# Fused attention and two gated layers: three raw-weight buffers, a single A22 buffer and weight units made at other steps

## The chip, the cores and the metric

The kernel is one program on one core of a Trainium2 chip. The metric is the device time of one execution in microseconds (us), from three runs. Engines are named as in the profile: PE (TensorE matmul), DVE (VectorE), ACT (ScalarE), POOL (GpSimd), SP (the engine whose queue issues the DMAs).

## The reference, cut to what matters

Three layers follow each other on 2304 tokens. The change lies in the third.

```
x  = attention(q, k, v, bias from positions)          # 4 x 8 heads, 576 positions, depth 64
h  = x @ w_in;  x = (h * cos(h)) @ w_out              # 512 -> 2048 -> 512
xn = x / sqrt(mean(x*x) + 1e-6) * rms_g
g, val = xn @ w_gate, xn @ w_val                      # 512 -> 1536, twice
out = (g / (1 + exp(-g)) * val) @ w_out               # 1536 -> 512
```

The weights arrive as 64-bit floats. On the chip each is made into a 32-bit float and then into a high and a low part, and each product is three matmuls (high by high, high by low, low by high).

## The kernel before

**Weights.** A piece is 128 x 512 weights, 512 KB raw. `w_dma` (L105) loads it on SP's queue into one of `NRAW` = 2 raw buffers. `w_abs` (L112, ACT) takes the absolute value of its upper words into one of `NW32` = 6 buffers named `w`. `w_conv` finishes it on DVE in four quarters (L123, L125, L127, L129); the last one frees the raw buffer, and `w_load` then asks for the next piece. Six pieces (two of gate, two of val, two of out) make a group.

**The third layer** runs in twelve groups, `run_group(p)`: groups 0 to 5 over 1024 tokens, 6 to 11 over 1024 others. A band of 256 tokens ("short") is fitted between in groups 1 to 5 and 7. In a group the gate and val products are seven products of half-sized blocks each (`gP1` to `gP7`, `vP1` to `vP7`, L974, six matmuls); `D0` to `D7` and `E0`, `E1` multiply what the group before made with its out weights (L1103, six matmuls), and `S0` to `S3` are the short products (L974 and L1078, tile `sh`). `steps(p)` fixes their order, in groups 2 to 5: gP1 gP2 D0..D7 E0 E1 vP1 vP2 gP6 gP7 vP6 vP7 S0 S1 gP5 vP5 gP3 S2 gP4 vP3 S3 vP4.

**Weight units.** In groups 0 to 5 the high and low parts, and sums of blocks, are made while the products run: `make` writes `g0 g1 g2 v0 v1 v2 o0 o1` and `gA`, `vA` (block A22, needed by P4 alone) with `halves` (a cast on ACT, L811, then a subtraction on POOL, L812), and `gS`, `vS` are four POOL operations in place (L927). `build` makes the first unit of a queue if its pieces are converted and its place is free, one per step. A22 has two buffers, `a0` and `a1`. The places are ten slots `wA`, `wB`, `wC`. `keep` stores each made unit to memory, from where groups 6 to 11 load it, so these make nothing.

**After a product**, `after` copies its sums out of PSUM on ACT, adds on DVE (`sums`, L1010) and multiplies (`times`, L986); `halves` makes the gated result `g` (ACT, then POOL). P3 adds into the same PSUM tile (`R`) that P5 filled, so gP3 waits for DVE's sum after gP5.

**Between them** stands a list `background`, one entry per step, for the 1/rms scaling of tokens that later groups use (blocks 2, 3 and 4): squares (ACT, L724) and their sums (DVE, L728), `rms_sum` (PE transposes into tile `sh`, shown as `ssp`, L734), `rms_mean` (DVE, then twelve small POOL operations, L749 to L752), `rms_back` (PE transposes into `sh`, shown as `rbp`, L759, and a copy to `rb` on ACT, L761), `rms_xn` (DVE, L766). `fit` and `mix` (L808) form operands for groups 6 to 11 in group 5, by the table `later2`.

What runs at a step of groups 0 to 5 is set in this order: the product, `after`, the table, `keep`, `build`, then `w_fill` (how many quarters is in `FILLS`), then `w_abs`:

```
x = wstate["abs"]
if x < wstate["dma"] and x < wstate["splitd"] + NW32 and tick[0] - asked.get(x, 0) >= 5:
    w_abs()
```

`tick` advances by 2 at a product and by 1 at other steps. Each engine works off its own list in order.

## Time and profile before

| | |
|---|---|
| median of 3 runs | 1179.1 us (1179.09 to 1179.51) |
| profiled execution | 1179.42 us |
| its span, first to last instruction | 1177.6 us |
| PE busy | 1123.0 us, 95% |
| DVE, ACT, POOL busy | 874.3, 606.7, 539.4 us |
| mean granted TensorE clock | 0.987 |

The page's slices show PE at 9 tenths or more nearly everywhere but between about 680 and 975 us, where it falls to 7 and 8; the granted clock dips to 8 in two slices there. That stretch is groups 0 to 5. A row of a timeline gives the start, the duration, the engine, line and operation with its tiles, and in brackets how long the engine had been idle and what ended it.

### The profile page before, as it was taken

Reading aid. Unit: us, or ns where it says so; the run is one execution under the profiler, and the core shown is the slowest. Engines: PE = TensorE matmul, PEld = TensorE weight load, DVE = VectorE, ACT = ScalarE, POOL = GpSimd, SP = SyncE. Lnnn points to the kernel's source line nnn. Section 1 sums busy time; section 2 is a strip of 40 time slices with the busy share of each in tenths; the row PEclk is TensorE's granted clock in tenths of the full one; section 3 lists DMA queues with packets and bytes.
Section 4 is the critical chain, followed back from the end, with each engine's and each line's share of the span. In section 5 each row is a group of like instructions: output and inputs, shape, how many; then the busy total and the mean of one; then the engine's idle time right before and its main releaser. Section 6 shows DMA issues by size and latency. Waiting matters only on the chain. (4 is left out here: it accounts for less than half of the span.)

```text
span 1177.6 us, 18893 instructions
## 1 busy us (share of the span) xinstructions
PE 1123.0 (95%) x6748; PEld 893.3 (76%) x6748; DVE 874.3 (74%) x1577; ACT 606.7 (52%) x1217; POOL 539.4 (46%) x649
## 2 busy tenths in 40 slices
...
GB/s 257 281 88 213 106 205 112 208 119 79 60 54 1 37 54 54 19 54 58 15 54 36 55 72 142 182 112 208 144 173 186 53 1 122 118 155 177 156 148 90
DMA packets 54286, 131.22 MB, mean 111 GB/s; under 512 B 8912, under 2 KB 15824, under 8 KB 54192
## 3 DMA queue, kind: packets, MB, share of 16 engines
...
q0 software_dynamic: 1584, 1.46, 0.8%
...
## 5 line engine op out<-in xcount | busy, mean ns | idle before, releaser
L678 POOL TENSOR_TENSOR g<-t,g 128x512 fp32r<-128x512 f32 (+1 forms) x80 | 98.7, 1234 | 233.4 <-ACT g L677 233.3
L812 POOL TENSOR_TENSOR g<-t,g 128x512 fp32r<-128x512 f32 (+1 forms) x60 | 76.0, 1267 | 219.0 <-ACT g L811 214.8
L627 PE MATMUL y<-g,wB 128*128 128x512 f32 (+1 forms) x600 | 132.0, 369 | 1.1 <-DVE yacc L712 1.1
L627 PEld LDWEIGHTS y<-g,wB 128*128 128x128 f32 x600 | 105.0, 189 | 20.3 <-DVE yacc L712 1.5
L264 DVE CUSTOM_DVE_ANT_0 e<-psS,bias 128x576 f32<-128x576 f32 x144 | 103.5, 752 | 22.6 <-PE psS L250 20.7
L273 ACT ACTIVATE e<-e,sm 128x576 f32<-128x576 f32 x144 | 111.3, 773 | 11.3 <-DVE sm L264 11.3
L627 PE MATMUL h<-xh,wB 128*128 128x512 f32 (+1 forms) x360 | 109.1, 369 | 0.0
L672 ACT ACTIVATE r<-r 128x512 f32<-128x512 f32 (+1 forms) x80 | 47.2, 590 | 118.8 <-DVE r L669 118.4
L1103 PE MATMUL y<-wC,g 128*128 128x512 f32 x300 | 86.9, 397 | 8.6 <-DVE yacc L1010 6.1
L677 ACT CAST g<-t 128x512 fp32r<-128x512 f32 (+1 forms) x80 | 46.2, 578 | 92.4 <-DVE t L676 86.1
L974 PE MATMUL Rg<-xh,wB 128*128 128x512 f32 x192 | 71.7, 415 | 18.5 <-DVE r L1010 17.7
L1103 PE MATMUL y<-wA,g 128*128 128x512 f32 x300 | 85.1, 392 | 0.0
L327 PE MATMUL o<-eT,v 128*64 128x256 f32 (+1 forms) x640 | 84.7, 411 | 0.0
L627 PE MATMUL y<-g,wC 128*128 128x512 f32 (+1 forms) x360 | 81.0, 375 | 3.8 <-POOL g L678 3.8
L811 ACT CAST g<-t 128x512 fp32r<-128x512 f32 (+1 forms) x60 | 34.7, 578 | 95.5 <-DVE t L986 95.5
L250 PE MATMUL psS<-kt,qt 64*128 64x288 f32 (+1 forms) x810 | 80.7, 309 | 0.8 <-DVE sm L264 0.7
L1010 DVE TENSOR_TENSOR yacc<-y,yacc 128x512 f32<-128x512 f32 (+1 forms) x81 | 54.5, 682 | 35.6 <-PE y L1103 35.5
L250 PEld LDWEIGHTS psS<-kt,qt 64*128 64x128 f32 (+1 forms) x810 | 62.5, 185 | 23.7 <-issue 8.5
L676 DVE TENSOR_TENSOR t<-r,h 128x512 f32<-128x512 f32 (+1 forms) x80 | 50.4, 630 | 34.9 <-ACT r L673 34.3
L627 PEld LDWEIGHTS y<-g,wC 128*128 128x128 f32 x360 | 63.6, 193 | 16.2 <-POOL g L678 4.0
L627 PEld LDWEIGHTS h<-xh,wB 128*128 128x128 f32 x360 | 65.8, 188 | 12.4 <-POOL wB L148 0.6
L1103 PEld LDWEIGHTS y<-wC,g 128*128 128x128 f32 x300 | 56.0, 190 | 24.1 <-DVE yacc L1010 8.6
(192 smaller groups left out, 2835.8 us busy)
## 6 DMA issues: line engine op xcount, KB each, us to landing
raw<-in_wf_dram SPq DMA_DIRECT2D x68, 512.0 KB, 3.7
wB<-kept SPq DMA_DIRECT2D x27, 512.0 KB, 4.2
kept<-wB SPq DMA_DIRECT2D x25, 512.0 KB, 2.7
...
kept<-wC SPq DMA_DIRECT2D x15, 512.0 KB, 3.0
wC<-kept SPq DMA_DIRECT2D x14, 512.0 KB, 4.3
...
```

Of the source, the lines that this page charges most:

```text
L250: nc.tensor.matmul(ps[:, x, 0:288], qt[r, a, 128 * p:128 * p + 128], kt[r, b_, k0:k0 + 288], start=(n == 0), stop=(n == len(terms) - 1), t ...
L264: nc.vector.tensor_tensor_reduce(out=e.rearrange("p (a b) -> p a b", a=2), in0=ps[:, :, 0:288], in1=bias_t[j].rearrange("p (a b) -> p a b" ...
L273: nc.scalar.activation(e, e, AF.Exp, bias=s_["m"][:, j:j + 1], scale=-1.0, accum_out=s_["sum"][:, j:j + 1])
L327: nc.tensor.matmul(o[64 * hh:64 * hh + 64, 0:n], vt[:, c, 64 * hh:64 * hh + 64], eT[:, 2 * c + (hh if c < 4 else 0), :], start=(c == 0), s ...
L627: nc.tensor.matmul(ps, a, b_, start=(first and k == 0), stop=(last and k == tot - 1))
L672: nc.scalar.activation(r, r, AF.Abs)
L676: nc.vector.tensor_tensor(t, r, ps, op=ALU.mult)
L678: nc.gpsimd.tensor_tensor(g[:, 1, :tn], t, g[:, 0, :tn].bitcast(F32), op=ALU.subtract)
L812: (eng or nc.gpsimd).tensor_tensor(lo, x, hi.bitcast(F32), op=ALU.subtract)
L974: nc.tensor.matmul(ps, w[:, a, cols], x[b](kt), start=(start and k == 0), stop=(k == n - 1), skip_group_check=not start)
L1010: nc.vector.tensor_tensor(to, x, y, op=ALU.add)
L1103: nc.tensor.matmul(y, g[a], o[:, b, cs], start=(n == 0), stop=(n == 5))
```

## The change

- The raw buffers become three and the `w` buffers five. `tick` advances by 1 at every step, and an absolute value comes at least six steps after its load was asked for.
- 1/rms is read by `rms_xn` from the PSUM tile it was transposed into; in the third layer the copy to `rb` goes.
- A22 has one buffer: `gA` and `vA` of a group are made after the group before has used its A22. The units' order becomes g0 v0 gA gS vA vS g1 g2 v1 v2. Groups 0 to 5 use nine slots.
- No quarter of a conversion at D2, D5, D7 (before: none at odd ones); one where there is something to convert at the other D and E steps.
- `rms_sum` of blocks 3 and 4 runs at D4 to gP7 only, `rms_back` at D2 to vP1 only.
- In group 5, operands are formed at other steps; the low part of T3 is made on DVE, and block 4's temporary lies in the buffers of the squares.
- The first partial results of a token block are copied from PSUM by DVE at even D, by ACT at odd D (before: all by ACT).

```
--- before.py
+++ after.py
@@ -33,8 +33,8 @@
 WB = 6
 WC = 3
 RING = WA + WB + WC
-NRAW = 2
-NW32 = 6
+NRAW = 3
+NW32 = 5
 SPL = 0
 LAG = 2
 NTT = S // 16
@@ -757,8 +757,10 @@
         ps = turn_tile("rbp")
         for t in range(0, tn, 128):
             nc.tensor.transpose(ps[:, t:t + 128], rst[bi][:, t // 128:t // 128 + 1].to_broadcast([128, 128]), ident)
-        rst[bi] = env["mp2"].tile([128, 512], F32, tag="rb", name="rb", bufs=1)[:, :tn]
-        nc.scalar.copy(rst[bi], ps[:, :tn])
+        rst[bi] = ps[:, :tn]
+        if env["psX"] is None:
+            rst[bi] = mp.tile([128, 512], F32, tag="u", name="rb", bufs=2)[:, :tn]
+            nc.scalar.copy(rst[bi], ps[:, :tn])
 
     def rms_xn(bi, d):
         t0, tn = BLKS[bi]
@@ -802,7 +804,7 @@
             todo = [((b_[:, hi], b_[:, hi], a[:, lo]), (a[:, hi], a[:, hi], b_[:, hi]))[k - 2]]
         else:
             if k == 2:
-                t2[:] = [rawp.tile([128, 512], I32, tag="w32", name="t2", bufs=NW32).bitcast(F32) for _ in range(2)]
+                t2[:] = [env["mp2"].tile([128, 512], F32, tag="sq", name="t2", bufs=2) for _ in range(2)]
             todo = [((t2[i], b_[:, 2 + i], a[:, i]), (a[:, 2 + i], a[:, 2 + i], t2[i]))[k - 2] for i in range(2)]
         for to, x, y in todo:
             nc.vector.tensor_tensor(to, x, y, op=ALU.subtract)
@@ -861,13 +863,13 @@
     tick = [0]
     mixed = {}
     asked = {}
-    ROLES = ("g0", "a0", "v0", "g1", "g2", "v1", "v2", "o0", "o1", "a1")
+    ROLES = ("g0", "a0", "v0", "g1", "g2", "v1", "v2", "o0", "o1")
     wr = {}
     free = dict.fromkeys(ROLES, 0)
     built = []
     units = {"G": [], "O": []}
     for q in range(PAIRS):
-        units["G"] += [(k, q) for k in ("gA g0 gS vA v0 vS g1 g2 v1 v2" if q else "g0 gA vA gS v0 vS g1 g2 v1 v2").split()]
+        units["G"] += [(k, q) for k in ("g0 v0 gA gS vA vS g1 g2 v1 v2" if q else "g0 gA vA gS v0 vS g1 g2 v1 v2").split()]
         units["O"] += [(k, q) for k in ("o0", "o1")]
     released = set()
 
@@ -885,7 +887,7 @@
         x = 2 if k[0] == "v" else 0
         if k[0] == "o":
             return base + 4 + int(k[1]), (k,)
-        return {"A": (base + x + 1, ("a%d" % (q % 2),)), "S": (base + x + 1, ())}.get(k[1], (base + x, (k,)))
+        return {"A": (base + x + 1, ("a0",)), "S": (base + x + 1, ())}.get(k[1], (base + x, (k,)))
 
     CLOSE = ("gP3", "S2", "gP4", "vP3", "S3", "vP4")
     OPEN = ("vP7", "S0", "S1", "gP5", "D0", "D1", "D2", "D3", "D4", "D5", "D6", "D7", "E0", "E1")
@@ -900,7 +902,7 @@
                 continue
             if q and (name in CLOSE or k[1] == "S" and name and name not in OPEN):
                 continue
-            if piece >= wstate["convd"] or any(r not in wr or free[r] < (q - 1 if r[0] == "a" else q) for r in roles):
+            if piece >= wstate["convd"] or any(r not in wr or free[r] < q for r in roles):
                 continue
             units[queue].pop(0)
             make(k, q)
@@ -928,10 +930,10 @@
             mixed[m, q] = tick[0]
         elif k[1] == "A":
             c = hi if m == "v" else lo
-            t = wr["a%d" % (q % 2)]
+            t = wr["a0"]
             halves(t[:, 0, c], t[:, 1, c], b[:, hi])
             if m == "v":
-                built.append((tick[0], "a%d" % (q % 2), q))
+                built.append((tick[0], "a0", q))
         else:
             halves(wr[k][:, 0], wr[k][:, 1], a if k[1] == "1" else b)
             w32_t.pop(x + int(k[1]) - 1)
@@ -943,7 +945,7 @@
         while wstate["split"] in released:
             wstate["split"] += 1
 
-    kept = dramp.tile([PAIRS - 1, len(ROLES) - 1, 128, 2, 512], F32, name="kept")
+    kept = dramp.tile([PAIRS - 1, len(ROLES), 128, 2, 512], F32, name="kept")
 
     def keep():
         while built and tick[0] - built[0][0] >= 4:
@@ -986,10 +988,10 @@
         nc.vector.tensor_tensor(t, t, val, op=ALU.mult)
 
     def part_a(p):
-        return "a%d" % (p % 2 if p < PAIRS else 1)
+        return "a0"
 
     def store_of(role):
-        return ROLES.index("a0" if role == "a1" else role)
+        return ROLES.index(role)
 
     def strassen(p, m, name):
         w, c0, x, bank, start = P[name]
@@ -1107,7 +1109,7 @@
             else:
                 to = oacc[bi].rearrange("p (d x) b -> p d (x b)", x=2)[:, d, cs]
             if first:
-                nc.scalar.copy(to, y)
+                (nc.scalar.copy if d % 2 else nc.vector.tensor_copy)(to, y)
             else:
                 sums(to, y, to)
             if last:
@@ -1149,8 +1151,8 @@
 
     later2[0] = {"gP2": [(fit, 1, "T1", nc.vector)], "gP7": [(fit, 1, "T4")]}
     later2[PAIRS - 1] = {"vP1": [(fit, 4, "B11")], "vP2": [(mix, 4, 0)], "gP6": [(fit, 4, "B21"), (mix, 4, 2)],
-                         "vP6": [(mix, 4, 3)], "vP7": [(fit, 4, "T2")], "S1": [(mix, 4, 1), (fit, 4, "T3")],
-                         "S2": [(fit, 4, "T1")], "S3": [(fit, 4, "B22")]}
+                         "vP7": [(fit, 4, "T2")], "S0": [(mix, 4, 1)], "vP5": [(fit, 4, "T3", nc.vector)], "S2": [(fit, 4, "T1")],
+                         "vP3": [(mix, 4, 3)], "S3": [(fit, 4, "B22")]}
     later2[PAIRS] = {"gP1": [(fit, 4, "T4")]}
     def steps(p):
         down = [f"D{k}" for k in range(8)] * (p > 0) + ["E0", "E1"] * (p - 1 in SHORT_IN)
@@ -1174,7 +1176,7 @@
     def run_group(p):
         todo, frees = steps(p)
         for i, name in enumerate(todo):
-            tick[0] += 2 if "P" in name else 1
+            tick[0] += 1
             if name == "L":
                 item_down(NI - 1)
                 st_psY.close()
@@ -1194,9 +1196,9 @@
             if p <= PAIRS:
                 keep()
                 build(name)
-                w_fill(FILLS.get(name, 1 - int(name[1]) % 2 if name[0] in "DE" else 1) if p else 2 if i > 3 else 0)
+                w_fill(FILLS.get(name, 0 if name in ("D2", "D5", "D7") else 1) if p else 2 if i > 3 else 0)
                 x = wstate["abs"]
-                if x < wstate["dma"] and x < wstate["splitd"] + NW32 and tick[0] - asked.get(x, 0) >= 5:
+                if x < wstate["dma"] and x < wstate["splitd"] + NW32 and tick[0] - asked.get(x, 0) >= 6:
                     w_abs()
                 for k in ("abs", "conv", "split"):
                     wstate[k + "d"] = wstate[k]
@@ -1204,7 +1206,9 @@
                 w_load()
                 asked.update((y, tick[0]) for y in range(x, wstate["dma"]))
                 if (p > 0 or i > 3) and background and not (p > 1 and background[0][0] in (rms_add, rms_xn) and name[0] in "DE" and int(name[1]) % 2 == 0) and not (
-                        p in SHORT_IN and background[0][0] in (rms_sum, rms_back) and name in ("S0", "S1", "gP5", "vP5", "gP3", "S2", "gP4", "vP3", "S3", "vP4")):
+                        p in SHORT_IN and (
+                        background[0][0] is rms_sum and name not in ("D4", "D5", "D6", "D7", "vP1", "vP2", "gP6", "gP7") or
+                        background[0][0] is rms_back and name not in ("D2", "D3", "D4", "D5", "D6", "D7", "vP1"))):
                     fn, *a = background.pop(0)
                     fn(*a)
                     if fn is rms_sum:
```

**POOL, group 4, from the subtraction for v0 on** (gate weights' w buffers are the first pair, val's the second; `wB`, `wC` are slots). Before:

```order
L812 TENSOR_TENSOR wB<-w_9397,wB 128x512
L927 TENSOR_TENSOR w_9419<-w_9419 128x256
L927 TENSOR_TENSOR w_9419<-w_9397,w_9419 128x256
L927 TENSOR_TENSOR w_9397<-w_9419,w_9397 128x256
L927 TENSOR_TENSOR w_9397<-w_9397 128x256
L812 TENSOR_TENSOR wB<-w_9262,wB 128x512
L812 TENSOR_TENSOR wB<-w_9272,wB 128x512
L812 TENSOR_TENSOR wC<-w_9397,wC 128x512
L812 TENSOR_TENSOR wC<-w_9419,wC 128x512
```

The change:

```order
L814 TENSOR_TENSOR wB<-w_9385,wB 128x512
L814 TENSOR_TENSOR wB<-w_9264,wB 128x256
L929 TENSOR_TENSOR w_9264<-w_9264 128x256
L929 TENSOR_TENSOR w_9264<-w_9252,w_9264 128x256
L929 TENSOR_TENSOR w_9252<-w_9264,w_9252 128x256
L929 TENSOR_TENSOR w_9252<-w_9252 128x256
L814 TENSOR_TENSOR wB<-w_9421,wB 128x256
L929 TENSOR_TENSOR w_9421<-w_9421 128x256
L929 TENSOR_TENSOR w_9421<-w_9385,w_9421 128x256
L929 TENSOR_TENSOR w_9385<-w_9421,w_9385 128x256
L929 TENSOR_TENSOR w_9385<-w_9385 128x256
L814 TENSOR_TENSOR wB<-w_9252,wB 128x512
```

The subtraction for gA, the four operations of gS and that for vA, which stood in the group before at gP7, gP5 and vP5, now stand between v0 and vS: g1 (the last row here, the sixth before) has ten instructions between v0 and itself where it had four. Behind it stand, in groups 2 and 4, the twelve small operations of `rms_mean`, then g2, v1 and v2. (The change's own lines have numbers two higher from L766 on.)

**DVE, group 2, from gP6's two quarters to the sum after gP5** (`r<-Rg`, the last row; `t<-t,sh` is the short band's product at S1). Before:

```order
L127 SCALAR_TENSOR_TENSOR w_8887<-raw,w_8887 128x512
L129 SCALAR_TENSOR_TENSOR w_8887<-raw,w_8887 128x512
L123 TENSOR_SCALAR w_9004<-w_9004 128x512
L125 TENSOR_SCALAR w_9004<-w_9004 128x512
L728 TENSOR_TENSOR sq<-sq 128x512
L127 SCALAR_TENSOR_TENSOR w_9004<-raw,w_9004 128x512
L129 SCALAR_TENSOR_TENSOR w_9004<-raw,w_9004 128x512
L123 TENSOR_SCALAR w_9029<-w_9029 128x512
L728 TENSOR_TENSOR sq<-sq 128x512
L986 TENSOR_TENSOR t<-t,sh 128x256
L125 TENSOR_SCALAR w_9029<-w_9029 128x512
L1010 TENSOR_TENSOR r<-Rg,r 128x512
```

The change:

```order
L127 SCALAR_TENSOR_TENSOR w_8894<-raw,w_8894 128x512
L129 SCALAR_TENSOR_TENSOR w_8894<-raw,w_8894 128x512
L123 TENSOR_SCALAR w_8906<-w_8906 128x512
L125 TENSOR_SCALAR w_8906<-w_8906 128x512
L127 SCALAR_TENSOR_TENSOR w_8906<-raw,w_8906 128x512
L129 SCALAR_TENSOR_TENSOR w_8906<-raw,w_8906 128x512
L988 TENSOR_TENSOR t<-t,sh 128x256
L123 TENSOR_SCALAR w_9017<-w_9017 128x512
L1012 TENSOR_TENSOR r<-Rg,r 128x512
```

The two sums of squares are gone from here (block 4's now run in group 3), and so are three quarters: none is left at vP7 and S0.

**ACT, group 2, from the cast for g1 to the copy of vP1's result** (`r<-Rv`; `L112` are absolute values). Before:

```order
L811 CAST wB<-w_8506 128x512
L811 CAST wB<-w_8546 128x512
L112 ACTIVATE w_8865<-raw 128x512
L811 CAST wC<-w_8612 128x512
L112 ACTIVATE w_8887<-raw 128x512
L811 CAST wC<-w_8642 128x512
L761 COPY rb<-rbp 128x512
L1110 COPY yaccs<-y 128x512 x2
L1016 COPY r<-Rv 128x512
```

The change:

```order
L813 CAST wB<-w_8512 128x512
L813 CAST wB<-w_8554 128x512
L112 ACTIVATE w_8881<-raw 128x512
L813 CAST wC<-w_8655 128x512
L112 ACTIVATE w_8894<-raw 128x512
L813 CAST wC<-w_8682 128x512
L112 ACTIVATE w_8906<-raw 128x512
L1112 COPY yaccs<-y 128x512
L1018 COPY r<-Rv 128x512
```

Three absolute values stand behind the casts for g2, v1 and v2, where there were two, behind those for g2 and v1. With six `w` buffers they took the buffers that g1 and g2 had been made from; with five they take those of g1, g2 and v1. All stand ahead of the copy that vP2's sum on DVE needs. The copy to `rb` is gone, and of the two copies of first partial results one is left.

## Rows read from the trace of the kernel before

**Rows 1.** Windows, groups 0 to 5 and 7; length, then busy PE, PEld, DVE, ACT, POOL, clock.
```profile
698.52:728.98 30.46, 23.74 (x99) 18.22 (x99) 23.73 (x31) 16.52 (x32) 19.67 (x16) 0.93 0.44 150
728.98:780.82 51.84, 40.13 (x183) 31.32 (x182) 38.30 (x54) 25.60 (x51) 34.01 (x39) 0.93 0.49 166
780.82:832.30 51.48, 44.44 (x202) 36.58 (x200) 39.80 (x59) 22.51 (x43) 30.61 (x37) 0.90 0.51 168
832.30:883.46 51.16, 42.35 (x202) 34.29 (x200) 39.75 (x56) 18.70 (x36) 29.30 (x36) 0.97 0.48 159
883.46:924.32 40.86, 39.05 (x193) 32.62 (x192) 30.76 (x45) 17.65 (x34) 26.84 (x24) 1.00 0.50 169
924.32:972.34 48.02, 41.03 (x194) 33.51 (x192) 29.55 (x36) 19.95 (x37) 36.99 (x28) 0.96 0.00 1
...
1004.98:1040.72 35.74, 35.74 (x182) 30.52 (x180) 7.82 (x11) 13.84 (x25) 7.06 (x6) 1.00 0.40 130
```

**Rows 2.** PE's waits in 698.5:972.4; us in total, times, longest.
```profile
PE Rg L974 <- DVE r L1010: 17.7, 5, 5.0
PE y L1103 <- DVE yacc L1010: 6.1, 6, 1.2
PE ssp L734 <- DVE t L986: 5.9, 2, 3.1
PE Xv L974 <- ACT wC L811: 4.9, 1, 4.9
```

**Rows 3.** The chain that ended last, group 7; start, us, what.
```profile
1007.86 10.88 PE y L1103 x48
```

**Rows 4.** PE timeline, group 2: the squares' transposes behind gP1.
```profile
785.41 1.12 PE L734 MATMUL ssp<-ident,sq 128*128 128x128 f32 x4 [3.07 <-DVE t L986]
```

**Rows 5.** ACT timeline, group 2: two absolute values.
```profile
800.52 0.67 ACT L112 ACTIVATE w<-raw 128x512 f32<-128x512 f32 x1 [6.58 <-POOL wB L812]
...
819.15 0.66 ACT L112 ACTIVATE w<-raw 128x512 f32<-128x512 f32 x1 [1.73 <-DMA raw<-in_wf_dram]
```

**Rows 6.** DVE timeline, group 2: quarters that wait, and the sum behind one.
```profile
801.22 0.79 DVE L123 TENSOR_SCALAR w<-w 128x512 f32<-128x512 f32 x1 [3.46 <-ACT w L112]
...
819.84 0.43 DVE L123 TENSOR_SCALAR w<-w 128x512 f32<-128x512 f32 x1 [0.99 <-ACT w L112]
...
821.63 0.68 DVE L1010 TENSOR_TENSOR r<-Rg,r 128x512 f32<-128x512 f32 x1
```

**Rows 7.** The page, DMA issues: count, KB, us to landing.
```profile
raw<-in_wf_dram SPq DMA_DIRECT2D x68, 512.0 KB, 3.7
```

**Rows 8.** POOL timeline, group 4: last gate subtraction, v0, then g1 and g2.
```profile
889.76 1.73 POOL L812 TENSOR_TENSOR g<-t,g 128x512 fp32r<-128x512 f32 x1 [1.28 <-ACT g L811]
891.46 1.30 POOL L812 TENSOR_TENSOR wB<-w,wB 128x512 fp32r<-128x512 f32 x1
...
895.85 2.55 POOL L812 TENSOR_TENSOR wB<-w,wB 128x512 fp32r<-128x512 f32 x2
```

**Rows 9.** POOL timeline, group 3: first and last of rms_mean's twelve operations.
```profile
842.41 0.20 POOL L749 TENSOR_TENSOR rsm<-rsm 128x4 f32<-128x4 f32 x1 [0.31 <-DVE rsm L747]
...
845.50 0.20 POOL L752 TENSOR_TENSOR rsm<-rsm 128x4 f32<-128x4 f32 x1
```

**Rows 10.** POOL timeline, group 4: subtraction for a 256-wide unit, nothing beside it.
```profile
887.74 0.74 POOL L812 TENSOR_TENSOR g<-t,g 128x256 fp32r<-128x256 f32 x1 [1.39 <-ACT g L811]
```

**Rows 11.** DVE timeline, group 4: a quarter beside POOL, then a first and a last quarter alone.
```profile
907.88 1.68 DVE L129 SCALAR_TENSOR_TENSOR w<-raw,w 128x512 int32<-128x512 int32 x1
910.59 0.43 DVE L123 TENSOR_SCALAR w<-w 128x512 f32<-128x512 f32 x1 [1.04 <-ACT w L112]
...
912.66 0.69 DVE L129 SCALAR_TENSOR_TENSOR w<-raw,w 128x512 int32<-128x512 int32 x1
```

**Rows 12.** POOL timeline, group 4: what ran beside the quarter of 907.88.
```profile
907.51 1.49 POOL L812 TENSOR_TENSOR g<-t,g 128x512 fp32r<-128x512 f32 x1 [1.28 <-ACT g L811]
```

**Rows 13.** DVE timeline, group 5: the two operations of one mix.
```profile
956.21 3.44 DVE L808 TENSOR_TENSOR yacc<-yacc,t 128x512 f32<-128x512 f32 x2 [1.20 <-POOL xl L812]
```

More of the change, by code (lines that the diff above doesn't have):

```diff
@@ L35 @@
 RING = WA + WB + WC
-NRAW = 2
-NW32 = 6
+NRAW = 3
+NW32 = 5
 SPL = 0
@@ L759, in rms_back @@
             nc.tensor.transpose(ps[:, t:t + 128], rst[bi][:, t // 128:t // 128 + 1].to_broadcast([128, 128]), ident)
-        rst[bi] = env["mp2"].tile([128, 512], F32, tag="rb", name="rb", bufs=1)[:, :tn]
-        nc.scalar.copy(rst[bi], ps[:, :tn])
+        rst[bi] = ps[:, :tn]
+        if env["psX"] is None:
+            rst[bi] = mp.tile([128, 512], F32, tag="u", name="rb", bufs=2)[:, :tn]
+            nc.scalar.copy(rst[bi], ps[:, :tn])
     def rms_xn(bi, d):
@@ L804, in mix @@
             if k == 2:
-                t2[:] = [rawp.tile([128, 512], I32, tag="w32", name="t2", bufs=NW32).bitcast(F32) for _ in range(2)]
+                t2[:] = [env["mp2"].tile([128, 512], F32, tag="sq", name="t2", bufs=2) for _ in range(2)]
             todo = [((t2[i], b_[:, 2 + i], a[:, i]), (a[:, 2 + i], a[:, 2 + i], t2[i]))[k - 2] for i in range(2)]
@@ L869, in attn_moe @@
     for q in range(PAIRS):
-        units["G"] += [(k, q) for k in ("gA g0 gS vA v0 vS g1 g2 v1 v2" if q else "g0 gA vA gS v0 vS g1 g2 v1 v2").split()]
+        units["G"] += [(k, q) for k in ("g0 v0 gA gS vA vS g1 g2 v1 v2" if q else "g0 gA vA gS v0 vS g1 g2 v1 v2").split()]
         units["O"] += [(k, q) for k in ("o0", "o1")]
@@ L902, in build @@
                 continue
-            if piece >= wstate["convd"] or any(r not in wr or free[r] < (q - 1 if r[0] == "a" else q) for r in roles):
+            if piece >= wstate["convd"] or any(r not in wr or free[r] < q for r in roles):
                 continue
@@ L944, in release @@
             wstate["split"] += 1
-    kept = dramp.tile([PAIRS - 1, len(ROLES) - 1, 128, 2, 512], F32, name="kept")
+    kept = dramp.tile([PAIRS - 1, len(ROLES), 128, 2, 512], F32, name="kept")
     def keep():
@@ L1109, in down @@
             if first:
-                nc.scalar.copy(to, y)
+                (nc.scalar.copy if d % 2 else nc.vector.tensor_copy)(to, y)
             else:
@@ L1151, in attn_moe @@
     later2[PAIRS - 1] = {"vP1": [(fit, 4, "B11")], "vP2": [(mix, 4, 0)], "gP6": [(fit, 4, "B21"), (mix, 4, 2)],
-                         "vP6": [(mix, 4, 3)], "vP7": [(fit, 4, "T2")], "S1": [(mix, 4, 1), (fit, 4, "T3")],
-                         "S2": [(fit, 4, "T1")], "S3": [(fit, 4, "B22")]}
+                         "vP7": [(fit, 4, "T2")], "S0": [(mix, 4, 1)], "vP5": [(fit, 4, "T3", nc.vector)], "S2": [(fit, 4, "T1")],
+                         "vP3": [(mix, 4, 3)], "S3": [(fit, 4, "B22")]}
     later2[PAIRS] = {"gP1": [(fit, 4, "T4")]}
@@ L1196, in run_group @@
                 build(name)
-                w_fill(FILLS.get(name, 1 - int(name[1]) % 2 if name[0] in "DE" else 1) if p else 2 if i > 3 else 0)
+                w_fill(FILLS.get(name, 0 if name in ("D2", "D5", "D7") else 1) if p else 2 if i > 3 else 0)
                 x = wstate["abs"]
-                if x < wstate["dma"] and x < wstate["splitd"] + NW32 and tick[0] - asked.get(x, 0) >= 5:
+                if x < wstate["dma"] and x < wstate["splitd"] + NW32 and tick[0] - asked.get(x, 0) >= 6:
                     w_abs()
```

18 lines of the change are left out of this document (10 added, 8 removed).

## The prediction

> **What bounds the kernel now.** I read the page first: PE is busy at 9 tenths or more in nearly every slice but between about 680 and 975 us. So I cut that stretch by groups of the third layer [rows 1]; the reader should set each length against PE's busy time in it. Groups 0 to 5 take 273.8 us and PE is busy for 230.7 of them: it idles 43.1. Group 7, whose weights all come from memory, has no idle at all in 35.74 us. A D or E step is 10.88 / 8 = 1.36 us [rows 3]; a product is also six matmuls, so the same; group 7's four S steps then take (35.74 - 22 x 1.36) / 4 = 1.46 each. Groups 2 to 5 have E0 and E1 beside group 7's steps: 35.74 + 2.72 = 38.46 undisturbed. Group 1 has 35.74, and group 0, with 14 products and a small step that I set at 1.4 (twelve narrow matmuls), 20.5. The losses over these are, by group, 10.0, 16.1, 13.0, 12.7, 2.4 and 9.6: 63.8 us. Idle makes 43.1 of it, a few transposes some 2, and the rest, about 19, is matmuls at the lower clock: in group 2 the granted clock is 0.90 (1.00 is 2.4 GHz, the other level 1.2 GHz), and PE is busy 6.0 us over the undisturbed length, after waits like the one of 3.07 [rows 1, 4].
>
> Then the list of PE's waits [rows 2]: 17.7 us go to five waits of gP3 for DVE's sum after gP5, 6.1 to six D or E steps whose PSUM tile DVE has not read yet, 5.9 to the squares' transposes, which need `sh` while DVE still owes a short product, and 4.9 (in group 1) to a v2 that is made late. The remaining idle lies mostly in group 0.
>
> The timelines say what makes DVE late. In group 2 an absolute value on ACT waits 1.73 for its raw load, the first quarter of its conversion waits behind it on DVE, and the sum that gP3 needs starts only at 821.63 [rows 5, 6]. In the D steps another absolute value waits for a `w` buffer that POOL has not released, and the quarter behind it stands on DVE in front of the sums of y [rows 5, 6]. Group 4 loses only 2.4: it has no rms work. That is my evidence that spreading the work is worth much.
>
> **The change part by part.** The sum is made against the profiled execution, 1179.4 us (span 1177.6), 0.3 above the median. T+ counts from the start of a group's gP1.
>
> *Raw loads.* With two buffers an absolute value came about three product steps after its load, 4.1 us, against 3.7 to landing [rows 7] and whatever SP's queue held before it. Six steps are 8.2. The store of a unit also comes four product steps after its making, not two, so SP stands less behind POOL. I take the load waits as gone in groups 2 to 4; conversions that are late then wait for POOL (below).
>
> *`rms_sum` to D4.* By D4 the short product of the group before is long read: the 5.9 go, with some 2.5 of half-speed matmuls behind the first. The transposes stay: 1.12 at the lower clock [rows 4], so about 0.5 a set.
>
> *Quarters at D steps.* D0 to D5 have none in groups 2 to 5, since all that has an absolute value is converted by then. The one at D6 waits, but only the sums of D7, E0 and E1 stand behind it, and three y tiles cover them. I take 5 of the 6.1 as gone; what is late next is the conversion itself, by vP2.
>
> *POOL's order.* gA, gS and vA now lie ahead of g1. Prices: a 512-wide unit 2.55 / 2 = 1.27; four mixing operations from 892.76 (891.46 + 1.30) to 895.85, 3.1; a 256-wide unit 0.74 [rows 8, 10]; `rms_mean` from 842.41 to 845.70, 3.3 [rows 9]. Before, POOL ended the last gate value at T+8.0 (889.76 + 1.73 - 883.46). The change takes the mixing away from DVE's last steps of a group, so I take T+6. Then v0 ends at 7.3, gA 8.0, gS 11.1, vA 11.9, vS 15.0, g1 16.3, g2 17.5, v1 18.8, v2 20.1. PE wants g1 at T+19.0 (2.72 + 13.6 + 2.72) and the others 1.36 apart, v2 at 23.1: no wait. With `rms_mean` behind g1 (groups 2 and 4) g2, v1 and v2 end at 20.8, 22.1 and 23.4, wanted with the transposes at 20.9, 22.3 and 23.6: just level.
>
> *ACT.* The third absolute value needs v1's `w` buffer, free at 18.8 in group 3 and at 22.1 in groups 2 and 4. Behind it stands the copy of vP1's result, done there by about 23.4, for which vP6 waits (it refills that tile from 22.3): 1.1; and vP2's sum, and then gP3, come late by up to 1. With transposes and a little half speed I give groups 2 and 4 a loss of 3.5 each. If POOL starts at T+8 as before, add 2 to each.
>
> *`rms_xn` from PSUM, and its place.* The ACT copy goes, 0.6 off PE's path: nothing. No row shows this operation with a PSUM input; the nearest are 0.69, a last quarter alone, and 1.68, one beside POOL [rows 11]. I take 0.74, nearer to a sum from PSUM at 0.68 [rows 6]. In group 3 DVE owes, from the first late quarter (POOL's g1 at 16.3, ACT 0.7 behind it: T+17) to gP5's sum: three sums of y, vP2's sum and product, the short product, the sum itself (4.5), three `rms_xn` (2.2), thirteen quarters (two of a piece at 0.43, two at 0.69: 7.3), three sums of squares (2.0): 16.0, so T+33.0. gP3 is due at 2.72 + 13.6 + 8.16 + 2.92 + 2.72 + 0.5 = 30.6. That is 2.4 of wait and 1.4 of half speed, with 1.5 at vP7 behind vP2's sum and the transposes a loss of 6 (0.5 to 10).
>
> *Group 5.* One mix of two operations, 3.44 [rows 13], moves behind gP5; block 4's four `rms_xn` and four late quarters come in, 3.0 and 2.2, partly in gaps between sums of y. gP3's wait falls from 5.0 [rows 2] to about 3; with half speed and transposes a loss of 5.5 (3 to 11).
>
> *Group 1.* v2 is made at D7 instead of gP6, but behind v0, gA, gS, vA and vS. POOL starts late there (the last gate value of group 0 at about T+9, I assume), so g1 ends near T+20 where PE wants it at 16.3: a wait of 4, where v2's alone was 4.9. Half of the first partial sums move from ACT to DVE at 0.68 each, so ACT falls less behind. gP3's wait stays at 3. Loss 11.5 (8 to 18).
>
> *Group 0.* One unit fewer beside T1's fit gains about 1; two quarters more before gP5's sum cost 0.9. Loss 9.5 (8 to 12).
>
> *Elsewhere* (attention, second layer, groups 6 to 11) PE is full before; a piece less is converted there, and the other moves touch nothing that PE waits for: nothing (0 to 1).
>
> The losses sum to 9.5 + 11.5 + 3.5 + 6 + 3.5 + 5.5 = 39.5, from 63.8: 24.3 gained, 1179.4 - 24.3 = 1155.1.
>
> **The rivals.**
> *PE's own pace.* Groups 0 to 5 fall to 30, 42, 39, 40, 39 and 40.5: 230.5, so 1136. For it: each engine by itself has less to do than PE. Against: a quarter that took 0.69 alone took 1.68 beside a POOL subtraction of 1.49 [rows 11, 12]; it ended when POOL did. Were that so for all such pairs, group 2 would hold POOL's 12 x 1.27 + 4 x 0.74 + 2 x 3.1 + 3.3 = 27.7 and DVE's six conversions and three products, 13.4 + 2.0, one after the other: 43.1, over PE's 38.46, and this rival falls. Group 4 of before has a like sum of 39.8 (no `rms_mean`) and took 40.86. I leave it 0.08.
> The Trainium skill (SBUF — State Buffer, "Who interferes with whom") has the rule: a DVE instruction with two SBUF inputs and a POOL instruction that reads SBUF shut each other out for their whole length. By that rule groups 2 and 4 cannot go much under 42 and the total not much under 1150; the trace agrees in the pair above.
> *DVE stays late at gP3.* The thirteen quarters crowd, or loads still land late: groups 2 and 4 then wait 3 and run 1.4 at half speed like the others (3.4 more each), groups 1, 3 and 5 1.3 more each: 10.7, so 1166. For it: what DVE owes in group 2 ends within 1 us of gP3. Chance 0.20.
> *ACT is held (slower).* Five `w` buffers chain ACT's copies to POOL's v1 and v2. It decides if v2 ends after T+23.5, so if v0 starts at T+9.4 and not 6, or if POOL's operations stretch as 1.73 for 1.27 does [rows 8]. With both, v0 starting at 9, v2 ends at 9 + 14.1 x 1.36 = 28, with `rms_mean` 31: waits of 5 and 8 in groups 2 to 5, 7.7 in group 1, 1.5 of half speed each, gP3 as before (4.4, in group 5 6.5). Groups 1 to 5 at 49.3, 52.4, 49.4, 52.4 and 51.5, group 0 at 30.5: 285.5, so 1191; with one of the two, near 1180. Against: the mixing that slowed DVE up to T+8 is gone. Chance 0.09.
> *Nothing comes of it*, what groups 2 and 3 win being lost in 1 and 5: 1179. Chance 0.03.
>
> **How the numbers follow.** The forecast, 1155, has 0.60, with bounds of its own at 1146 and 1164. The range goes down to 1144 for part of the first rival, and up to 1171 for the second and for POOL at T+8 throughout; most of the first rival and the last two lie outside. A measurement of this kernel tells 0.2% (2.4 us) from no change. Faster: 0.60 + 0.20 + 0.08; same 0.03; slower 0.09.
>
> **What would show it.** Right: no wait of the squares' transposes for DVE; ACT's waits for raw loads under 2 us in all of groups 2 to 4; waits of D and E steps under 2; groups 2 and 4 near 42 us, group 3 near 44.5. Wrong: PE waits for vP1's copy or vP2's sum of over 3 us in each group, a clock under 0.95 in groups 2 and 4, group 1 above 50 or group 5 above 46.

## The result and the profile after

The changed kernel takes 1163.1 us (median of four runs, 1163.06 to 1165.01) against 1179.3 for the kernel before: a ratio of 0.9865, 95% interval 0.9848 to 0.9882. So 16.2 us were won where 24.3 were forecast. The profiled execution of the change took 1165.0 (span 1163.2), 1.9 above its median, so groups are compared with groups below. The stretch ahead of group 0 ends between 696.3 and 699.1 in the executions compared here, and group 0 takes between 30.9 and 33.0 where its code is the same, so a total is good to some 2 us only.

Windows of the change over groups 0 to 5 (length; then busy PE, PEld, DVE, ACT, POOL; granted clock; DMA share; GB/s), which answer to [rows 1]:

```profile
699.09:730.66 31.57, 24.71 (x99) 19.12 (x99) 22.79 (x33) 17.51 (x33) 19.36 (x15) 0.88 0.48 166
730.66:776.64 45.98, 40.05 (x184) 31.91 (x182) 37.61 (x59) 22.72 (x47) 30.51 (x35) 0.96 0.52 164
776.64:823.02 46.38, 40.23 (x198) 32.80 (x196) 35.66 (x53) 18.84 (x36) 29.18 (x36) 1.00 0.57 185
823.02:869.26 46.24, 41.27 (x197) 34.32 (x196) 36.19 (x55) 20.27 (x39) 25.82 (x24) 0.96 0.54 173
869.26:913.17 43.91, 41.41 (x197) 34.11 (x196) 34.91 (x51) 17.73 (x34) 28.99 (x36) 0.96 0.52 170
913.17:957.94 44.77, 42.12 (x198) 35.58 (x197) 32.85 (x42) 20.18 (x39) 38.24 (x32) 0.92 0.00 1
```

A group's loss is what it takes over its undisturbed length (20.5, 35.74, then four times 38.46):

| group | 0 | 1 | 2 | 3 | 4 | 5 | sum |
|---|---|---|---|---|---|---|---|
| loss before | 10.0 | 16.1 | 13.0 | 12.7 | 2.4 | 9.6 | 63.8 |
| loss forecast | 9.5 | 11.5 | 3.5 | 6.0 | 3.5 | 5.5 | 39.5 |
| loss measured | 11.1 | 10.2 | 7.9 | 7.8 | 5.5 | 6.3 | 48.8 |

Of the 9.3 us that are missing, groups 2 and 4 hold 6.4. Group 4, the best one before, became 3 us longer.

A single group's length is less certain than this table looks. In a later run (group 5's table as before) the work of group 3 is the same and gP3 waits the same 2.05 us, but there the product behind it takes 2.6 us where it takes 1.5 in the change; its first matmul in the change, then in that run:

```profile
860.77 0.50 PE L976 MATMUL Rg<-xh,wB 128*128 128x512 f32 x1 [2.05 <-DVE r L1012]
```

```profile
860.30 0.64 PE L976 MATMUL Rg<-xh,wB 128*128 128x512 f32 x1 [2.05 <-DVE r L1012]
```

Group 3 took 46.2 us (granted clock 0.96) in the one and 47.8 (0.93) in the other, and group 4 43.9 (0.96) and 42.3 (1.00). So a difference of up to some 1.6 us in one group can be the clock alone.

PE's waits in groups 0 to 5 of the change (us in total, times, longest), which answer to [rows 2]:

```profile
PE Rg L976 <- DVE r L1012: 7.8, 3, 4.5
PE Xv L976 <- DVE r L1012: 6.0, 3, 2.9
PE Rv L976 <- ACT r L1018: 4.2, 3, 1.7
PE y L1105 <- DVE yacc L1012: 2.7, 1, 2.7
PE sh L976 <- DVE xl L814: 2.5, 3, 1.2
...
PE Xg L976 <- POOL wB L814: 1.3, 2, 0.7
```

The wait of the squares' transposes is gone, and of gP3's 17.7 us 7.8 are left, 4.5 of them in group 0. New are the third and the last line, and the second, which was one wait of 1.9 in group 0, has grown: vP7 waits for vP2's sum (2.9 in group 3, 2.7 in group 5), vP6 for ACT's copy of vP1's result (1.7 each in groups 2 and 4), gP7 for the unit g2 (0.56 and 0.72 there). POOL's timeline of group 2 (T = 776.64) shows where the last two come from: the last gate value, v0, then g1, the first and two later operations of `rms_mean`, and g2.

```profile
783.10 1.46 POOL L814 TENSOR_TENSOR g<-t,g 128x512 fp32r<-128x512 f32 x1 [1.28 <-ACT g L813]
784.52 1.71 POOL L814 TENSOR_TENSOR wB<-w,wB 128x512 fp32r<-128x512 f32 x1
...
794.74 1.29 POOL L814 TENSOR_TENSOR wB<-w,wB 128x512 fp32r<-128x512 f32 x1
795.98 0.20 POOL L749 TENSOR_TENSOR rsm<-rsm 128x4 f32<-128x4 f32 x1
...
799.58 0.63 POOL L751 TENSOR_SCALAR rsm<-rsm 128x4 f32<-128x4 f32 x1
800.30 0.20 POOL L752 TENSOR_TENSOR rsm<-rsm 128x4 f32<-128x4 f32 x1
800.45 1.28 POOL L814 TENSOR_TENSOR wB<-w,wB 128x512 fp32r<-128x512 f32 x1
```

v0 starts at T+7.9 and not at T+6, `rms_mean` takes 4.5 us and not 3.3, and g2 ends at T+25.1 instead of 20.8; the rest of that difference, 1.2, went between v0's start and g1's end (11.5 and not 10.3). ACT's timeline of the same group shows what stands behind it: the short band's SiLU at the start, then the second absolute value and the copy of vP1's result.

```profile
779.72 0.38 ACT L1086 ACTIVATE t<-sh 128x256 f32<-128x256 f32 x1 [1.40 <-POOL g L814]
...
801.76 0.68 ACT L112 ACTIVATE w<-raw 128x512 f32<-128x512 f32 x1 [4.53 <-POOL wB L814]
...
804.06 0.58 ACT L1018 COPY r<-Rv 128x512 f32<-128x512 f32 x1
```

The absolute value needs the `w` buffer that POOL's subtraction for g2 frees at 801.7; the copy, whose input is ready since vP1's last matmul ended at 798.05, comes 6 us later. The first row matters as much: the SiLU waits for a POOL subtraction, because both use the two buffers named `t`. Behind the SiLU stand DVE's product, then DVE's sum of vP4, ACT's cast and POOL's last gate value, and only then v0. The list of ACT's waits of the kernel before had that wait already:

```profile
ACT t L1084 <- POOL g L812: 4.4, 4, 1.4
```

**Theory A:** POOL's list from v0 to v2 starts late (the chain through `t`) and is stretched by `rms_mean`; ACT and PE wait for it. **Theory B:** DVE has too much to do between vP1 and gP5, and POOL's order does not matter.

### The profile page after: what moved, and what is told of

Read it like the earlier page. It is cut to its first block, busy times and chain, and to the rows that moved or that the text cites. A ratio compares the mean times of both kernels' runs of the same rounds, so it can differ in the third digit from the quotient of the medians.

```text
span 1163.2 us, 18903 instructions
## 1 busy us (share of the span) xinstructions
PE 1122.3 (96%) x6748; PEld 894.8 (77%) x6748; DVE 873.6 (75%) x1588; ACT 600.6 (52%) x1205; POOL 533.3 (46%) x647
## 5 line engine op out<-in xcount | busy, mean ns | idle before, releaser
L677 ACT CAST g<-t 128x512 fp32r<-128x512 f32 (+1 forms) x80 | 46.2, 578 | 88.0 <-DVE t L676 77.7
L976 PE MATMUL Rg<-xh,wB 128*128 128x512 f32 x192 | 69.1, 401 | 9.6 <-DVE r L1012 7.8
L287 PE MATMUL pt<-ident,e 128*128 128x128 f32 x576 | 73.4, 277 | 0.4 <-ACT e L273 0.3
```

What stands on the lines that cost most here:

```text
L287: nc.tensor.transpose(pt[:, 128 * i:128 * i + 128], e[:, k0:k0 + 128], ident)
L976: nc.tensor.matmul(ps, w[:, a, cols], x[b](kt), start=(start and k == 0), stop=(k == n - 1), skip_group_check=not start)
```

## The experiments

All are compared with the kernel before on the same chip (1179.9 to 1180.2 us in these runs) and with the change at 1163.1, which was measured beside 1179.3 for the kernel before: so a difference from the change is uncertain by another 0.6 to 0.9 us. The ratios are those to the kernel before, with their 95% intervals. The diffs show only the lines that matter.

### POOL's list

**rms_mean behind v2.**

```diff
+        rst[bi] = ms, r, q2
+        if bi <= 2: rms_newton(bi)
+    def rms_newton(bi):          # the twelve POOL operations
-  (rms_sum, b), (rms_mean, b)] + [(quiet,)] * 6
+  (rms_sum, b), (rms_mean, b)] + [(quiet,)] * 5 + [(rms_newton, b)]     # blocks 3 and 4
```

> The change, but in groups 2 and 4 the twelve small POOL operations of rms_mean are issued at vP1, behind the subtraction for v2, instead of at D4 between g1 and g2. Theory A (POOL's list is late, and ACT and PE wait for it): PE's waits of 0.56 and 0.72 us at gP7 and of 1.72 and 1.67 at vP6 in groups 2 and 4 go, with some half-speed matmuls; groups 2 and 4 fall from 46.4 and 43.9 us to about 43.5 and 41.5, the total from 1163.1 to about 1158. Theory B (DVE has too many quarters between vP1 and gP5, POOL's order does not matter): the wait only moves to vP7 or gP3, where DVE's sums are late; total within 1.5 us of 1163.1.

Measured: 1155.8 (0.9794, 0.9777 to 0.9810). Windows of groups 2 and 4:

```profile
776.00:819.92 43.92, 41.05 (x197) 34.00 (x196) 35.30 (x53) 19.11 (x37) 30.89 (x36) 0.96 0.58 197
865.88:906.28 40.40, 39.58 (x198) 33.00 (x196) 32.30 (x51) 17.80 (x34) 31.24 (x36) 1.00 0.54 185
```

Groups 2 and 4 fall by 2.5 and 3.5 us, the others stay within 0.3 but for group 0; the waits at gP7 and vP6 in groups 2 and 4 are gone, and vP7 in group 4 gets 0.7. Theory A. (Of the 7.3 between the medians these two groups explain 6.0.)

**The short SiLU in a tile of its own.**

```diff
-            t = new("t")[:, 0:256]
+            t = scratch[0].bitcast(F32)[:, i, 0:256]      # half of the tenth weight slot
```

> The change, but the short band's SiLU writes into a tile of its own (half of the unused tenth weight slot) instead of one of the two buffers named t. Theory A (POOL begins v0 at T+7.2 to T+7.9 because a chain runs through these two buffers: a POOL subtraction must free t before ACT's SiLU, before DVE's product, before DVE's sum of vP4): ACT's waits of 1.4 us for POOL before each SiLU of the short band at the start of groups 2 to 5 go, v0 starts about 1.4 earlier, D3's wait of 2.66 in group 2 goes; 1 to 1.5 us less in each of groups 2 to 5, so about 1158. Theory B (DVE is what is late): D3's wait goes, the rest is found again at vP7 and gP3; about 1161.

Measured: 1159.4 (0.9835, 0.9813 to 0.9856). ACT's SiLU and POOL's v0 in group 2 (T = 775.26):

```profile
776.84 0.38 ACT L1086 ACTIVATE wB<-sh 128x256 f32<-128x256 f32 x1
```

```profile
782.18 1.71 POOL L814 TENSOR_TENSOR wB<-w,wB 128x512 fp32r<-128x512 f32 x1
```

The SiLU waits for nothing now and v0 starts at T+6.9, 1.0 earlier (T+6.2, 4.4 and 6.2 in groups 3 to 5). Groups 2, 4 and 5 win 1.0, 2.6 and 2.2; group 3 loses 0.5: its vP7 waits 2.1 instead of 2.9, its gP3 3.6 instead of 2.1. The chain is shown; the gain is between the two theories, and in group 3 the waits go as theory B has it. The gains of single groups are less sure: in groups 4 and 5 the granted clock is 1.00 here and 0.96 and 0.92 in the change, and PE's busy time, not its waits, makes 1.9 and 2.6 of the difference. The worth of the tile is better read from totals, 3.7 here and 3.8 on top of the first experiment (next run). And D3's wait in group 2, which both theories saw gone, keeps 1.7 of its 2.7:

```profile
PE y L1105 <- DVE yacc L1012: 1.7, 1, 1.7
```

**Both.**

> rms_mean's POOL operations behind v2 and the short SiLU in a tile of its own, together. Theory A (both shorten POOL's list, at its start and in its middle): rms_mean gave 2.5 and 3.5 us in groups 2 and 4, the own tile 1.0, -0.5, 2.6 and 2.2 in groups 2 to 5; with g2 no longer late in group 4 the two overlap there (group 4 cannot fall under 38.5), so 8 to 10 in all and a total near 1154 to 1155; groups 2 and 4 near 43 and 39.5. Theory B (DVE's crowd takes over): no more than the better of the two alone, 1155.8 to 1157, with gP3's waits in groups 2 to 5 above 8 us together.

Measured: 1152.0 (0.9768, 0.9753 to 0.9783), with the 1152.3 below the fastest here. Windows of groups 2 to 5:

```profile
774.69:816.41 41.72, 39.90 (x198) 32.86 (x196) 35.82 (x53) 18.87 (x36) 31.47 (x36) 1.00 0.61 206
816.41:863.19 46.78, 41.04 (x198) 34.42 (x196) 37.60 (x57) 21.22 (x41) 27.00 (x25) 0.96 0.56 179
863.19:902.29 39.10, 39.10 (x198) 33.10 (x196) 31.72 (x49) 16.92 (x33) 29.87 (x36) 1.00 0.51 182
902.29:944.61 42.32, 39.53 (x198) 33.02 (x196) 33.73 (x42) 20.11 (x40) 37.96 (x31) 1.00 0.00 1
```

The gains add (11.1 us against 7.3 and 3.7 alone), which is more than theory A gave. In group 4 PE does not idle at all, 0.6 over the undisturbed 38.46. Group 3 is left with 8.3 us of loss.

### DVE's list in group 3

**Quarters behind vP2's sum**, on top of both:

```diff
-    FILLS = {"gP1": 2, "vP1": 2, "gP6": 2,
+    FILLS = {"gP1": 2, "vP1": 0, "vP2": 3, "gP6": 2,
```

> As the run before, and the two quarters at vP1 move to vP2 (0 at vP1, 3 at vP2, where there was 1), so that in DVE's list vP2's sum stands ahead of them. The wait left at vP7 in groups 3 and 5 (2.1 and 1.9 us for vP2's sum): Theory C (the sum stands behind quarters whose absolute values and raw words are late; the work itself has room): vP7's waits fall under 1 us, gP3's do not grow, 2 to 4 us less than the run before. Theory B (DVE simply has too much to do before gP3): what vP7 wins gP3 loses, within 1 us of the run before.

Measured: 1154.5 (0.9790, 0.9774 to 0.9806), 2.5 slower. vP7's waits fall from 2.2 and 1.6 to 1.3 and 0.9, gP3's rise from 3.6 and 1.2 to 4.2 and 3.1 (groups 3, 5). Theory B for these two waits; that the total would lose 2.5 neither theory said, and the two intervals just overlap.

**Block 4's squares from gP3 on**, on top of both:

```diff
+  p == 3 and background[0][0] in (rms_sq, rms_add) and name in ("vP1", "vP2", "gP6", "gP7", "vP6", "vP7", "S0", "S1", "gP5", "vP5") or
```

> The run with both parts (rms_mean's POOL operations behind v2, an own tile for the short SiLU), and in group 3 the squares of block 4 and their three sums run from gP3 on instead of from vP2 to S1. Theory B for group 3 (what DVE owes ahead of gP5's sum sets its length; three sums are 2.04 us of it): gP3's wait of 3.58 falls to about 1.5, with a little half speed 2 to 3 us less in group 3, at most 1 more in group 4; 1149.5 to 1150.5. Theory A (late absolute values, not the amount of work): gP3's wait stays above 3, total within 1 us of 1152.0.

Measured: 1152.3 (0.9766, 0.9751 to 0.9780). Windows of groups 3 and 4:

```profile
817.69:860.13 42.44, 39.53 (x198) 33.01 (x196) 34.85 (x52) 18.89 (x36) 25.56 (x24) 1.00 0.57 186
860.13:903.59 43.46, 41.16 (x198) 34.09 (x196) 35.26 (x55) 19.19 (x37) 31.61 (x36) 0.96 0.51 175
```

Group 3 wins 4.3 us, gP3's wait falls from 3.6 to 0.8; but group 4 loses 4.4, with a wait of 2.3 at D3 for DVE's sums of y. In DVE's timeline the second and third of the moved sums now stand ahead of the sum of group 4's gP2 and of the sums of y, the third stretched to 1.77:

```profile
863.02 0.68 DVE L728 TENSOR_TENSOR sq<-sq 128x512 f32<-128x512 f32 x1
...
866.34 1.77 DVE L728 TENSOR_TENSOR sq<-sq 128x512 f32<-128x512 f32 x1
868.04 0.68 DVE L1018 TENSOR_TENSOR r<-Xg,r 128x512 f32<-128x512 f32 x1
868.64 1.87 DVE L1018 TENSOR_TENSOR yacc<-y,yacc 128x512 f32<-128x512 f32 x3
```

Group 3 went as theory B has it, and the total did not move: what was taken out of it made the next group late instead. The four squares on ACT moved along with their three sums on DVE, so which of the two group 3 was waiting for is not shown.

### Parts of the change undone, one at a time

**Steps of rms_sum and rms_back as before.**

```diff
-  background[0][0] is rms_sum and name not in ("D4", ..., "gP7") or background[0][0] is rms_back and name not in ("D2", ..., "vP1")
+  background[0][0] in (rms_sum, rms_back) and name in ("S0", "S1", "gP5", "vP5", "gP3", "S2", "gP4", "vP3", "S3", "vP4")
```

> The change, but rms_sum and rms_back may run at the steps where they ran before (anywhere but at S0 to vP4). The prediction's term (two waits of the squares' transposes, 5.9 us, and 2.5 at half speed behind them): about 6 to 8 us come back, 1169 to 1171. Rival (the transposes' wait was DVE's lateness at the start of the group, which is owed at D3 anyway): 2 to 3 us come back, 1165 to 1166. It also puts rms_mean ahead of v0 and g1 on POOL, which by theory A alone would cost 1 to 2 us more in groups 2 and 3 or 4.

Measured: 1167.7 (0.9899, 0.9884 to 0.9913), 4.6 back, between the two forecasts. By groups: 2 loses 5.4, 3 loses 1.5, 4 wins 2.7. PE's waits:

```profile
PE Rg L976 <- DVE r L1012: 11.0, 4, 4.5
PE Xv L976 <- DVE r L1012: 8.2, 5, 3.4
PE ssp L734 <- DVE t L988: 2.9, 2, 2.4
```

The transposes' wait comes back at half its old size, and gP3 and vP7 wait longer, so the 4.6 is not the worth of that wait alone. Group 4's gain is that of the first experiment: the step at D4 put `rms_mean` into POOL's list there, and gave back part of what it won.

**Two raw buffers** (`NRAW = 2`, absolute values at least three steps behind their loads, five `w` buffers).

> The change with two raw buffers and absolute values three steps behind their loads; still five w buffers. The prediction's step (the loads were late with two buffers, and ACT and then DVE waited): ACT's waits for raw loads come back (8.6 us in six waits before, none with three buffers), gP3's waits grow by 1 to 3 us in each of groups 2 to 4, 1167 to 1171. Rival (with five w buffers ACT waits for POOL's release anyway, so that a load has time): ACT's waits for loads under 3 us, total within 2 us of 1163.1.

Measured: 1169.1 (0.9907, 0.9892 to 0.9921), 5.9 back. ACT's wait and, behind it, PE's:

```profile
ACT w L112 <- DMA raw<-in_wf_dram: 20.5, 13, 4.0
```

```profile
PE Rg L976 <- DVE r L1012: 19.6, 6, 4.0
```

As the prediction's step has it, with more than twice the 8.6 that ACT waited for loads before; gP3 waits 3.4 to 4.0 in groups 1 to 4.

**The same with six `w` buffers.**

> The same with six w buffers, the buffers of the kernel before. Theory A (POOL's list holds ACT through the w buffers): with a sixth buffer the absolute values of a group no longer wait for v1's release, ACT's waits for POOL fall from 28 us to under 15, the waits at vP6 and vP7 in groups 2 to 5 (9 us) shrink by 3 to 5, so 3 to 5 us less than the run before, and if raw loads cost little, faster than the change: 1158 to 1162. Rival (absolute values only wait somewhere else, now for loads): within 1.5 us of the run before or slower.

Measured: 1165.1 (0.9872, 0.9857 to 0.9886), 4.0 less than the run before, so with two raw buffers the sixth `w` buffer is worth 4. That is theory A's drop, but not its total of 1158 to 1162, and ACT's waits for POOL's release fall only from 28.6 to 23.8, not under 15. Three raw and five `w` buffers are 2.0 ahead of two and six, which the intervals do not tell from nothing (0.9848 to 0.9882 and 0.9857 to 0.9886): the third raw buffer was paid for with most or all of its worth. (The steps between a load and its absolute value, six or three, went with the number of raw buffers; they were not tried apart.)

**A22 in two buffers, units in the old order.**

```diff
-   "g0 v0 gA gS vA vS g1 g2 v1 v2" if q
+   "gA g0 gS vA v0 vS g1 g2 v1 v2" if q
-   t = wr["a0"]
+   t = wr["a%d" % (q % 2)]
```

> The change, but A22 has two buffers again and the units stand in the order gA g0 gS vA v0 vS g1 g2 v1 v2, so that gA, gS and vA of a group are made in the group before. Theory A (POOL's list between v0 and v2 is what groups 2 to 5 wait for): with four operations less there g1 to v2 are 4 to 5 us earlier, the waits at gP7, vP6 and vP7 in groups 2 to 5 (9.5 us) go; 1155 to 1160. Theory B (POOL's mixing beside DVE's last quarters of a group is what made gP3 late): gP3 waits 2 to 3 us in each of groups 1 to 5 again; 1168 to 1172.

Measured: 1177.7 (0.9975, 0.9965 to 0.9986), 14.6 back. PE's waits:

```profile
PE y L1105 <- DVE yacc L1012: 14.8, 9, 2.8
PE Rg L976 <- DVE r L1012: 13.0, 5, 4.5
PE Rg L976 <- ACT wB L813: 4.7, 1, 4.7
PE Rg L976 <- POOL wB L814: 3.4, 1, 3.4
```

Both theories missed: theory A's gain did not come, and gP3 waits no more than 3.8 in any group but 0. The loss is in group 1's first product, which waits 8.1 for g0, and at D7 in groups 3 to 5 (2.3 to 2.8 each) and E0 in groups 2 and 4 (1.1 each). There a quarter stands on DVE, in front of the sums of y, and waits for an absolute value on ACT that waits for POOL; in group 4:

```profile
892.82 0.67 ACT L112 ACTIVATE w<-raw 128x512 f32<-128x512 f32 x1 [4.74 <-POOL wB L814]
```

```profile
893.52 0.78 DVE L123 TENSOR_SCALAR w<-w 128x512 f32<-128x512 f32 x1 [4.67 <-ACT w L112]
```

**The same with two raw and six `w` buffers.**

> The change with A22 in two buffers and the old order of the units, and also two raw and six w buffers with absolute values three steps behind their loads: what is left of the change are the steps of rms_sum and rms_back, 1/rms from PSUM, group 5's table, the quarters at D steps and the first copies. Theory P (the two-buffer A22 only hurts because five w buffers are too few for units that stand open across two groups): much of the 14.6 us that it cost with five w buffers goes; 1166 to 1171. Theory Q (the mixing at the end of the group before, beside DVE's last quarters, is itself what costs): 1175 to 1180, and gP3's waits of 10 us or more in groups 1 to 5.

Measured: 1176.5 (0.9965, 0.9952 to 0.9978). Theory Q by its time, 11.4 above the run with six buffers and the new order. Its reason isn't shown by it: gP3 waits 20.2 here, but 17.3 there as well. The loss isn't in the same places either: with five `w` buffers groups 0 and 1 took 9.7 of it, with six group 2 takes 6.0 and group 3 3.2. Group 2 here, then in the run with six buffers and the new order:

```profile
778.86:832.28 53.42, 44.65 (x197) 36.19 (x196) 38.92 (x58) 20.60 (x39) 31.65 (x38) 0.90 0.55 182
```

```profile
778.15:825.60 47.45, 42.62 (x197) 35.41 (x196) 38.86 (x54) 19.79 (x38) 30.32 (x37) 0.93 0.57 190
```

So the single A22 with the new order is worth 11 to 15 us with either set of buffers, the largest part of the change, by two different ways, and what is left without it and without the buffers gains 3.7 us over the kernel before. Whether A22's place or the order of the units does it was not tried apart.

**Group 5's table as before.**

```diff
-  "vP7": [T2], "S0": [mix 1], "vP5": [T3 on DVE], "S2": [T1], "vP3": [mix 3]
+  "vP6": [mix 3], "vP7": [T2], "S1": [mix 1, T3], "S2": [T1]
```

> The change with group 5's table of mixes and fits as before (one mix back from vP3 to vP6, another with T3's fit back at S1, T3's low part on POOL). The prediction's step (one mix of 3.44 us moved behind gP5): gP3's wait in group 5, none in the change, comes back at 3 to 5 us with some half speed; group 5 at 48 to 51, the total at 1166.5 to 1169. Rival (DVE's quarters of the next pieces make group 5 long, not the mixes): within 1.5 us of 1163.1.

Measured: 1169.0 (0.9906, 0.9891 to 0.9921), 5.9 back. Group 5 takes 49.4, gP3 waits 4.0 in it (none in the change), as forecast; the total lies at the upper edge of the forecast.

**First partial results on ACT.**

```diff
-                (nc.scalar.copy if d % 2 else nc.vector.tensor_copy)(to, y)
+                nc.scalar.copy(to, y)
```

> The change with all first partial results copied on ACT again. The prediction's step for group 1 (ACT falls less behind when half of them go to DVE): 0.5 to 2 us come back in group 1, 1163.6 to 1165. Rival (what group 1 waits for is the units on POOL and the short band's fit on DVE; on DVE the four copies cost as much as they give on ACT): within 0.5 us, or up to 1 us faster.

Measured: 1164.9 (0.9874, 0.9857 to 0.9890). Group 1 loses 0.6, group 6 0.8 (a wait of 0.45 at D3); within the forecast, but as small as the scatter of a total. Inconclusive beyond "under 2 us". Groups 3 to 6 make none of these copies, and they differ from the change by as much or more (group 5 by 1.2, at clock 1.00 against 0.92).

Undone one at a time, the parts cost 4.6, 2.0 (both buffers together), 14.6, 5.9 and 1.8 us, 28.9 in sum, where the whole change gained 16.2: they are not independent, and none of these prices is a share of the 16.2.

## Why the prediction came out as it did

- **Raw loads:** right. None of ACT's waits is for a load (six, 8.6 us, before). The price, the `w` buffer given up for it, stands in the prediction only as the delay of 1.1 at vP6 and in the slower rival; the runs put it at 4.0 with two raw buffers.
- **A22:** its single buffer and the new order, the largest part when undone (11 to 15 us), have no term of their own in the sum. They enter it as v0's earlier start, as operations ahead of g1 and as group 1's wait for it; a gain of that size is nowhere in it, and what makes it stays open.
- **rms_sum to D4:** the 5.9 went; undone, groups 2 and 3 lose 6.8, against 8.4 forecast (5.9 and 2.5 of half speed), but only 2.9 of it is that wait. That `rms_mean` would then stand between g1 and g2 on POOL was seen, and called level.
- **POOL's order, the step that failed:** "The change takes the mixing away from DVE's last steps of a group, so I take T+6." v0 starts at T+7.9, 7.2, 6.9 and 7.1 in groups 2 to 5. What holds it is the chain through the two `t` buffers, which has nothing to do with the mixing; with an own tile v0 starts 0.9 to 2.6 earlier, in group 2 at T+6.9, so that half of its 1.9 has another cause. The second half of the failure is `rms_mean`, priced at 3.3 and measured at 4.0 and 4.5 beside DVE. The prediction's "If POOL starts at T+8 as before, add 2 to each" would have given groups 2 and 4 5.5 each; they lost 7.9 and 5.5.
- **ACT:** the mechanism was right, the size was not: vP6's wait for vP1's copy was put at 1.1 and is 1.7. It is the slower rival in small: v2 ends at T+27.8 and T+25.7 in groups 2 and 4 (the second of the two subtractions into `wC` that stand behind g2's), past its T+23.5, but there PE waits 2.3 and 2.4 us for POOL and ACT, not 8.
- **D steps:** 5 of 6.1 were to go; 2.7 are left, and 0.8 in group 1 for the copies that DVE now makes. The 2.7 are group 2's D3: its sums stand behind the short product, which waits 1.9 for the SiLU, and behind four quarters from the group's start, not behind one of a D step; without the wait for the SiLU 1.7 stay.
- **Group 3:** gP3's wait 2.4 forecast, 2.05 measured; vP7's 1.5 forecast, 2.9 measured; the loss 6 forecast, 7.8 measured. `rms_xn` from PSUM takes 0.73 to 0.74, as estimated (0.74).
- **Group 5:** the loss fits (5.5 and 6.3), the place does not: no wait at gP3, 2.65 at vP7. Group 1 likewise (11.5 and 10.2): g1's wait is 1.3, not 4, gP3's is none, not 3, and 3.0 go to S0, which waits for the fit of the short band, most of it on DVE. In both groups the loss came out nearly right by luck.
- **Group 0:** gP3's wait grew by 1.2 (0.9 forecast, for two quarters); a gain of about 1 for the unit that is no longer made beside T1's fit was forecast. vP7's wait fell by 1.5 (from 1.9 to 0.4), but gP5 and vP5 now wait 0.6 and 1.3 for ACT's copies, so nothing of it is left.
- **PE's own pace:** the argument against it took too much. Its pair does not end together, as it says: the quarter ends at 909.56, 0.56 behind POOL's subtraction at 909.00, as if it had run behind it. Then it let all of DVE's quarters and products exclude POOL's work, which gave 43.1 for group 2 as a floor. With POOL's list mended groups 2 and 4, which hold the same operations, take 41.7 and 39.1, and 40.3 and 38.9 with the quarters moved. That single pairs do exclude each other is seen below; so the sum overcounts, by what was not settled. Half of its quarters (L123, L125) read one SBUF input; without them it would be 27.7 + 8.3 + 2.0 = 38.0, under PE's 38.46, but some of these stretch too (below). The 42 that was worked out by the Trainium skill's rule (SBUF — State Buffer, "Who interferes with whom") is refuted for these groups as well; the rule for a pair is not.

DVE stays late at gP3, the second likeliest, is nearer to the measured time (1166), but not to where it was lost: of its waits of 3 in groups 2 and 4 there are 1.2 and none.

Of the signs named beforehand two came (no wait of the transposes for DVE, none of ACT for loads) and three did not: D steps wait 3.5 and not under 2, groups 2 and 4 take 46.4 and 43.9 and not 42, group 3 46.2 and not 44.5. None of the signs of being wrong came. So the total lies in the forecast's range while two of its steps, POOL's order and the D steps, did not happen as told.
